# Quarter sums of two weights: a queue of their own and places of their own, in place

## The chip, the cores and the metric

The kernel runs on one core of one Trainium2 chip. The metric is the device time of one execution in microseconds (us). Before the change the median of three runs is 793.73 us (792.7 to 794.22).

## What is computed

```python
attn = softmax(cap * tanh(q @ k.T / sqrt(64) / cap))        # 4 x 12 heads, 448 tokens, 64 wide
x = (attn @ v) laid out as 1792 tokens x 768
h = ((x @ w1) * (x @ w2)) @ w3 @ w_out                       # 768 -> 1024 -> 1024 -> 768
h = h @ w_in                                                 # 768 -> 1024
solu = h * softmax(h)
ln = (solu - mean) / sqrt(var + 1e-6) * g_ln
out = ln @ w_out2                                            # 1024 -> 768
```

All inputs are float32. The kernel makes each float32 matmul from three products of a high and a low part (the high part is a cast to fp32r, the low part what remains): `THREE` names the pairs.

## The kernel before

The program has four stages, and TensorE works through them one after the other.

1. Attention runs by pairs of heads, and between its matmuls TensorE folds w3, w_out and w_in into one 1024 x 1024 weight (`fold`, L743), which lands in DRAM as `w_dr`. The order of all engines is written out there by a planner (`Order`) that keeps its own clock of what is due.
2. The gated products (`products`, L1108, matmul L1119) multiply the attention output by w1 and w2, in blocks f = 0 to 7 of 128 columns of each. The tokens come in four batches of 448; the first pass takes batches 0 and 1 for each f in turn, and a short second pass takes batches 2 and 3 for two blocks. A block's weight tile `wt` has two buffers; it is filled by three pieces of 512 columns (`plan_w`), each loaded as 512 KB into a landing tile `ld` (three of them), converted by three VectorE operations (L328, L331, L334) into one of two `cv` tiles, cast by ScalarE (L340, the high part) and subtracted by VectorE (L349, the low part). Piece 0 holds the columns that the block's first matmuls need. Once attention ends, about 365 us into the span, the order is no longer written out: the loop at L1304 emits 18 matmuls, then steps of the queues, and the framework's scheduler places the instructions of each engine, by its own estimate of when each can start, with the emission order as rank.
3. Six blocks (`multiply`, L1323) do the other batches with Strassen-like sums of tokens and weights: seven products each, whose operands are prepared beforehand. `first_set` combines the first block's weights (`set0`), `two_three` (T) and `one_four` (U) combine the tokens.
4. The last two weights (the folded `w_dr` and w_out2 times g_ln, `wg_dr`) are applied in the same manner (`product`, L1426), first with seven operands ws1 to ws7, later with seven wg.

A DRAM weight is taken as a 2 x 2 grid of quarters, and four of the seven operands need sums of quarters. These are made in stage 2: `plan_sums` loads all four quarters of one row block, subtracts four times on VectorE and stores four sums into `tw_dr` (t) or `tg_dr` (tg). Before the change each row block is done as two halves of the columns, so there are eight items t(0) to t(7) and eight items tg(0) to tg(7).

The work of stage 2 stands in queues of class `Ahead`: items are loaded up to `depth` ahead of the one in work, strictly in the order in which they were added. `ahead` holds almost all of it, `xq` the tokens. In `ahead`, after block 5's pieces: `plan_last(5)` (w_out2's block g5, converted through the same landing tiles and stored to `wg_dr`), set0's load, t(0) and t(1), block 6's pieces (w6), g6, t(2) to t(4), block 7's pieces (w7), g7, t(5) to t(7), `first_set`, tg(0) to tg(3), T, the load and split of ws1 (`plan_block`), tg(4) to tg(7), U, the load of ws2, set1. The sums land in the same three `ld` tiles as the weights, and their results go to four `ts` tiles. Each piece of w6 waits until block 4 is through, each of w7 until block 5 is.

All of these transfers but the tokens' factors (`rb`, issued by GpSimd) are issued by SP, in one queue. Besides the loads it carries the stores of the sums, of the products (`ab_dr`, L1147), of g (`wg_dr`, L655), and a 1.5 MB store of each block's split weight for later use (`w12_dr`, L1149).

Of the kernel before, what the change touches and what calls it, by code (L numbers as in the profile page):

```python
# [9 lines left out]
F32 = mybir.dt.float32  # L10
F32R = mybir.dt.float32r
U32 = mybir.dt.uint32
AF = mybir.ActivationFunctionType
ALU = mybir.AluOpType
# [4 lines left out]
P = 128  # L19
B, H, S, D = 4, 12, 448, 64  # L20
# [221 lines left out]
def attention_moe_solu(ctx: ExitStack, tc: tile.TileContext, q, k, v, cap, w12, w3t, wo, win, wout2, g_ln, out):  # L242
# [49 lines left out]
    ahead, xq = Ahead(LANDS, order), Ahead(1, order)  # L292
# [4 lines left out]
    def since(test):  # L297

        met = []

        def when():
            if not met and test():
                met.append(order.now)
            return met[0] if met else None
        return when

    def landing(i, src, n, kind):
        t = conv.tile([P, 2 * HALF], U32, tag="ld", bufs=LANDS, name=f"ld{i}")
        lands[i] = t[:, :n].bitcast(kind)
        dst = lands[i]  # L310
        if len(src.shape) == 3:
            dst = dst.rearrange("p (a b) -> p a b", a=src.shape[1])
        elif len(src.shape) == 4:
            dst = dst.rearrange("p (a b c) -> p a b c", a=src.shape[1], b=src.shape[2])
            for g in range(src.shape[1]):
                sync.dma_start(out=dst[:, g], in_=src[:, g])
            return
        sync.dma_start(out=dst, in_=src)
# [552 lines left out]
    def four(dr, i, part, n):  # L871

        return dr[i][:, :, :, part * n:(part + 1) * n]
# [4 lines left out]
    def summed(i, t_dr, i_, part, n, m, t):  # L878

        if m == 0:  # L880
            t.append(lands.pop(i).rearrange("p (g h n) -> p g h n", g=2, h=2))
        b = t[0]
        t.append(place["ts"].tile([P, HALF], F32, tag="ts", bufs=4, name=f"t{i}_{m}")[:, :2 * n].rearrange("p (t n) -> p t n", t=2))
        if m == 0:
            dve.tensor_tensor(t[1][:, 0], b[:, 0, 1], b[:, 0, 0], ALU.subtract)
            dve.tensor_tensor(t[1][:, 1], b[:, 1, 1], t[1][:, 0], ALU.subtract)
        else:
            dve.tensor_tensor(t[2][:, 0], b[:, 1, 1], b[:, 0, 1], ALU.subtract)
            dve.tensor_tensor(t[2][:, 1], b[:, 1, 0], t[1][:, 1], ALU.subtract)
        sync.dma_start(out=t_dr[2 * m:2 * m + 2, :, i_, part * n:(part + 1) * n].rearrange("t p n -> p t n"), in_=t[-1])  # L890

    def plan_sums(kind, dr, t_dr, i_, part, n):

        i = len(ahead.items)

        def rest():
            t = []
            for m in range(2):
                summed(i, t_dr, i_, part, n, m, t)
        ahead.add((kind, i_, part), lambda: landing(i, four(dr, i_, part, n), 4 * n, F32), list, lambda: [("none", 0, 0, 0, rest)], None, lambda: 0.0 if "ts" in place else None)  # L900
# [18 lines left out]

    def second(m):  # L920
        if m not in ws:
            ws[m] = both_.tile([P, 2, NF // 2, HALF], F32R, tag="many", name=f"ws{m}")
        return ws[m]

    def plan_block(m, part):
        there = since(lambda: "ws" in place)
        ahead.add(("f", m, part), lambda: block_load(m, part, W4, tw_dr, second(m)), list,
                  lambda: [("none", 0, 0, 0, lambda: block_split(ws[m], part))], None, there)
# [79 lines left out]
    def plan_plain(key, do, test, load=lambda: None):  # L1008
        ahead.add(key, load, list, lambda: [("none", 0, 0, 0, do)], None, since(test))
# [27 lines left out]
    halves_ = [(i_, part) for i_ in range(NF // 2) for part in range(2)]  # L1037

    def plan_t(*items):
        for k in items:  # L1040
            plan_sums("t", W4, tw_dr, *halves_[k], HALF // 2)

    def plan_tg(*items):
        for k in items:
            plan_sums("tg", G4, tg_dr, *halves_[k], DM // 4)
# [13 lines left out]
    plan_last(5)  # L1059
    plan_plain("set0", lambda: None, lambda: "set" in place, lambda: load_set(0))  # L1060
    plan_t(0, 1)
    plan_w(6)
    plan_last(6)
    plan_t(2, 3, 4)
    plan_w(7)
    plan_last(7)
    plan_t(5, 6, 7)
    plan_plain("first set", first_set, lambda: "set" in place and ("x", B - 1, NPAIR // 2 - 1) in xq.done)
    plan_tg(0, 1, 2, 3)
    for c in range(NC // 2):  # L1070
        plan_plain(("T", c), lambda c=c: two_three(c), lambda: (NF - 1, 0) in fin)
    for part in range(2):
        plan_block(EARLY[0], part)
    plan_tg(4, 5, 6, 7)
    for c in range(NC // 2):
        plan_plain(("U", c), lambda c=c: one_four(c), lambda: (NF - 1, 1) in fin)
    plan_plain(("f", EARLY[1]), lambda: None, lambda: "ws" in place, lambda: block_load(EARLY[1], None, W4, tw_dr, second(EARLY[1])))
# [221 lines left out]
    place["ws"] = ws = {EARLY[0]: wsp.tile([P, 2, NF // 2, HALF], F32R, tag="w1", name="ws1")}  # L1299
# [4 lines left out]
    while fill(18 * 201):  # L1304
        ahead.step(3)
        xq.step(1)
    while xq.step(1):
        pass
    while ahead.step(1):
        pass  # L1310
# [82 lines left out]
    for part in range(2):  # L1393
        plan(1 + part, 3, (high_w, ws, EARLY[1], part))
        plan(1 + part, 4, (low_w, ws, EARLY[1], part))
# [227 lines left out]
    plan(0, 3, (high_w, ws, 5, 0), (low_w, ws, 5, 0), (high_w, ws, 5, 1), (low_w, ws, 5, 1), (high, 0, 4), (high_w, ws, 4, 0), (sum4, 0))  # L1623
# [125 lines left out]
```

## Time and profile before

| | us |
|---|---|
| median of three runs | 793.73 |
| the profiled execution, its own time | 794.05 |
| its span, first to last instruction | 792.3 |
| TensorE busy | 772.7 |
| VectorE busy | 617.1 |
| ScalarE busy | 442.3 |

The span is what the instructions cover; the 1.75 us between it and the execution's time lie around it. Busy times are sums over the span: an engine can be 98% busy and still work at half its clock for a while, which the granted clock shows. An idle stretch has a releaser, the instruction or transfer that came last among those waited for. Names of tiles are the program's without their numbers, so the DRAM tensors `w_dr` and `w12_dr` both read `w_dr`, and `in_w12` reads `in_w`.

### The profile page before, as it was taken

What the parts mean: (1) busy time and instruction counts of PE and PEld (TensorE: products, weight loads), DVE (VectorE), ACT (ScalarE), POOL (GpSimd) and SP (SyncE); (2) the same over time, 40 slices, a digit from 0 to 9 for tenths busy, and PEclk for the clock granted to TensorE, in tenths of its full rate; (3) what the DMA queues carried; (4) which work ended last, traced back from release to release, by engine and by line L of the source; (5) the groups of instructions that cost most, each with busy time, mean ns of one, the idle gap of its engine ahead of it and who ended that gap; (6) DMA issues with size and microseconds to landing.
All of it is one profiled execution on the core that took longest, in us unless ns stands there. A gap on an engine that the chain in (4) does not pass through costs nothing.

```text
span 792.3 us, 11304 instructions
## 1 busy us (share of the span) xinstructions
PE 772.7 (98%) x3956; PEld 613.7 (77%) x3956; DVE 617.1 (78%) x1132; ACT 442.3 (56%) x656; POOL 55.0 (7%) x106
## 2 busy tenths in 40 slices
PE   9999999999999999999986998999999999999998
PEld 6546666876867676767986997998788888899998
DVE  6995795798999469965777978877886668978972
ACT  6887766357577767672222313324576666845642
POOL 0110000000110112001000000000011111100000
PEclk9999999999999999999998999999999999999999
DMA  8776465586996665647978797545743345996432
GB/s 288 249 226 225 126 216 171 183 259 224 324 316 219 217 207 180 187 160 270 326 269 303 247 308 248 168 149 181 238 151 115 107 99 130 274 198 132 138 93 80
DMA packets 150920, 162.46 MB, mean 205 GB/s; under 512 B 66324, under 2 KB 122832, under 8 KB 149840
## 3 DMA queue, kind: packets, MB, share of 16 engines
q1 hardware_dynamic: 148128, 155.91, 61.9%
q0 software_dynamic: 2592, 5.73, 2.9%
q8 instruction: 31, 0.51, 0.3%
q14 instruction: 25, 0.20, 0.1%
q10 hardware_dynamic: 144, 0.10, 0.0%
HBM read 114.04 MB, written 47.53 MB: 204 GB/s over the span
## 4 chain that ended last, share of the span: by engine, by line
PE 76%; DMA 9%; DVE 8%; ACT 4%; issue 2%; SPq 0%; DVEq 0%; ACTq 0%
PE u L1434 14%; PE o L523 9%; PE f L771 8%; PE f L755 8%; PE ab L1119 7%; PE v L1434 7%; PE sc L442 6%; PE us L1331 5%; PE y L1434 4%; PE n L523 2%; PE sc L438 2%; PE vs L1331 2%; DMA ld<-in_w 2%; DMA tg_dr<-t 2%; DMA ws<-w_dr 1%
## 5 line engine op out<-in xcount | busy, mean ns | idle before, releaser
L1119 PE MATMUL ab<-xs,wt 128*128 128x448 f32 x720 | 152.7, 370 | 8.3 <-ACT wt L340 8.3
L1119 PEld LDWEIGHTS ab<-xs,wt 128*128 128x128 f32 x720 | 137.2, 192 | 24.3 <-ACT wt L340 9.0
L455 ACT ACTIVATE sc<-sc,small 128x896 f32<-128x896 f32 (+1 forms) x96 | 82.8, 888 | 47.7 <-PE sc L442 42.0
L460 ACT ACTIVATE p<-sc,small 128x896 f32<-128x896 f32 (+1 forms) x96 | 84.5, 921 | 0.6
L1434 PE MATMUL u<-ws,a 128*128 128x512 f32 x336 | 80.7, 391 | 0.7 <-DVE ws L1375 0.5
L523 PE MATMUL o<-p,vd 128*64 128x448 f32 x384 | 77.5, 545 | 0.0
L1434 PEld LDWEIGHTS u<-ws,a 128*128 128x128 f32 x336 | 62.8, 188 | 15.0 <-DVE ws L1375 1.2
L755 PE MATMUL f<-w,w_o 128*128 128x512 f32 x288 | 70.7, 396 | 0.0
L771 PE MATMUL f<-w_i,w 128*128 128x512 f32 x288 | 68.1, 392 | 0.1
L755 PEld LDWEIGHTS f<-w,w_o 128*128 128x128 f32 x288 | 53.2, 188 | 16.3 <-issue 3.4
L771 PEld LDWEIGHTS f<-w_i,w 128*128 128x128 f32 x288 | 53.5, 188 | 14.2 <-issue 2.7
L1434 PE MATMUL u<-wg,a 128*128 128x384 f32 x336 | 62.0, 334 | 0.0
L1434 PEld LDWEIGHTS u<-wg,a 128*128 128x128 f32 x336 | 58.5, 188 | 0.4 <-DVE a L1569 0.3
L523 PEld LDWEIGHTS o<-p,vd 128*64 128x64 f32 x384 | 25.4, 136 | 41.2 <-issue 40.3
L334 DVE SCALAR_TENSOR_TENSOR cv<-ld,cv 128x512 uint32<-128x512 uint32 (+1 forms) x80 | 52.1, 658 | 0.8
L331 DVE SCALAR_TENSOR_TENSOR cv<-ld,cv 128x512 uint32<-128x512 uint32 (+1 forms) x80 | 51.9, 660 | 0.9
L1565 ACT CAST a<-s 128x512 fp32r<-128x512 f32 (+1 forms) x42 | 31.2, 755 | 30.5 <-DVE s L1587 17.9
L481 DVE TENSOR_TENSOR s<-p,p 128x896 f32<-128x896 f32 x18 | 19.6, 1091 | 32.8 <-ACT p L460 18.1
L328 DVE TENSOR_SCALAR cv<-ld 128x512 uint32<-128x512 uint32 (+1 forms) x80 | 32.2, 406 | 12.7 <-DMA ld<-in_w 6.0
L1434 PE MATMUL v<-ws,a 128*128 128x512 f32 x168 | 40.7, 390 | 0.5 <-DVE ws L1375 0.5
L1569 DVE TENSOR_TENSOR a<-s,a 128x512 fp32r<-128x512 f32 (+1 forms) x42 | 35.4, 851 | 6.5 <-ACT a L1565 6.4
L1434 PEld LDWEIGHTS v<-ws,a 128*128 128x128 f32 x168 | 31.5, 188 | 7.4 <-DVE ws L1375 0.9
(188 smaller groups left out, 1300.4 us busy)
## 6 DMA issues: line engine op xcount, KB each, us to landing
ld<-in_w SPq DMA_DIRECT2D x24, 512.0 KB, 5.0
w_dr<-wt SPq DMA_DIRECT2D x6, 1536.0 KB, 6.7
q<-w_dr SPq DMA_DIRECT2D x24, 384.0 KB, 4.1
ld<-in_w3t SPq DMA_DIRECT2D x16, 512.0 KB, 4.5
w_dr<-e SPq DMA_DIRECT2D x28, 256.0 KB, 3.5
ldx<-ab_dr SPq DMA_DIRECT2D x14, 512.0 KB, 4.1
c_dr<-h SPq DMA_DIRECT2D x14, 512.0 KB, 2.6
ldx<-c_dr SPq DMA_DIRECT2D x56, 128.0 KB, 3.2
```

The costliest lines, as they stand in the source:

```text
L331: dve.scalar_tensor_tensor(d[1], d[0][:, :, 1], 0xC0000000, d[1], ALU.bitwise_and, ALU.bitwise_or)
L334: dve.scalar_tensor_tensor(d[1], d[0][:, :, 0], 29, d[1], ALU.logical_shift_right, ALU.bitwise_or)
L442: pe.matmul(sc[:, j, :S], keys[rows], qq[rows, :], start=(m == 0), stop=(m == len(terms) - 1))
L455: act.activation(sc[:, :w, :S], sc[:, :w, :S], AF.Tanh, scale=qscale)
L460: act.activation(p, sc[:, :w, :S], AF.Exp, scale=capt)
L523: pe.matmul(dst[i * width:(i + 1) * width, :S], weights, moving, start=first, stop=stop)
L755: pe.matmul(banks_[c][0], lw[:, a], fw["3", h, g][:, e], start=begins, stop=(g == NF - 1 and m == 2))
L771: pe.matmul(begun_[m_][0], w34[m_][:, a, c, :], rw[:, e], start=(c == 0 and m == 0), stop=(c == NC - 1 and m == 2))
L1119: pe.matmul(pp[f, b, i][0][:, :S], w[:, u], xs[b, c][:, e], start=begins, stop=(c == NC - 1 and m == 2))
L1331: pe.matmul(pu[g], w[:, u, c * P:(c + 1) * P], moved(m, c)[:, e], start=(begins and c == 0 and i == 0), stop=(c == NC // 2 - 1 and i == 2) ...
L1434: pe.matmul(banks[g], a[r][m][:, p, k * P:(k + 1) * P], b[m][:, e, k, :], start=(first and k == 0 and i == 0), stop=(k == NF // 2 - 1 and ...
L1569: dve.tensor_tensor(lo, source(r, m), raw(hi), ALU.subtract)
```

## The change

- A third queue `tq` of depth 2 takes the sums, set0's load, T, `first_set`, U, the loads of ws2 and ws1, and set1. `ahead` keeps the blocks and g: after block 5's pieces come g5, g6, w6, g7, w7.
- Sums are made per row block at full width: four items t and four tg, each loaded by two transfers (each with both halves of one row of quarters), four subtractions in place (512 or 384 columns wide), two stores of two sums each.
- They land in places of their own: one tile `big` in the space of the former `ts` tiles, and two halves of the tile that later becomes ws1 (`within`). The order of places is big, half 0, half 1, big for t, and half 0, half 1, big, half 0 for tg.
- ws1 is loaded at the end of `tq`, and its split moves from stage 2 into blocks 3 and 4 of stage 3, in the steps where ws2's split stands in blocks 1 and 2.
- The loop of stage 2 takes 2 steps of `ahead`, 1 of `xq` and 2 of `tq` per 18 matmuls, where it took 3 and 1.
- In stage 4 the first half of ws5 is split one step sooner (step 2 of the first round).

```diff
-    ahead, xq = Ahead(LANDS, order), Ahead(1, order)
+    ahead, xq, tq = Ahead(LANDS, order), Ahead(1, order), Ahead(2, order)
...
-    def plan_sums(kind, dr, t_dr, i_, part, n):
-
-        i = len(ahead.items)
+    def plan_sums(kind, dr, t_dr, i_, n, home):
+
+        t = []
+
+        def load():
+            t.append(home(f"{kind}{i_}")[:, :4 * n].rearrange("p (g n) -> p g n", g=4))
+            for g in range(2):
+                sync.dma_start(out=t[0][:, 2 * g:2 * g + 2], in_=dr[i_][:, g])
 
         def rest():
-            t = []
-            for m in range(2):
-                summed(i, t_dr, i_, part, n, m, t)
-        ahead.add((kind, i_, part), lambda: landing(i, four(dr, i_, part, n), 4 * n, F32), list, lambda: [("none", 0, 0, 0, rest)], None, lambda: 0.0 if "ts" in place else None)
+            b = t.pop()
+            for to, x, y in ((0, 1, 0), (1, 3, 1), (3, 3, 0), (2, 2, 3)):
+                dve.tensor_tensor(b[:, to], b[:, x], b[:, y], ALU.subtract)
+            for m, two in ((0, b[:, ::3]), (2, b[:, 1:3])):
+                sync.dma_start(out=t_dr[m:m + 2, :, i_, :].rearrange("t p n -> p t n"), in_=two)
+        tq.add((kind, i_), load, list, lambda: [("none", 0, 0, 0, rest)], None, lambda: 0.0 if "ts" in place else None)
...
     def plan_plain(key, do, test, load=lambda: None):
-        ahead.add(key, load, list, lambda: [("none", 0, 0, 0, do)], None, since(test))
+        tq.add(key, load, list, lambda: [("none", 0, 0, 0, do)], None, since(test))
...
+    def apart(name):
+        return place["ts"].tile([P, 4 * HALF], F32, tag="big", name=name)
+
+    def within(k):
+        def home(name):
+            if "first" not in homes:
+                homes["first"] = wsp.tile([P, 2, 4 * HALF], F32, tag="w1", name="sums")
+            return homes["first"][:, k]
+        return home
+
+    def begin_weight(m):
+        ws[m] = (wsp if m == EARLY[0] else both_).tile([P, 2, NF // 2, HALF], F32R, tag="w1" if m == EARLY[0] else "many", name=f"ws{m}")
+        block_load(m, None, W4, tw_dr, ws[m])
...
-    plan_last(5)
+    for f in range(5, NF):
+        plan_last(f)
+        if f > 5:
+            plan_w(f)
+    for i_, home in enumerate((apart, within(0), within(1), apart)):
+        plan_sums("t", W4, tw_dr, i_, HALF, home)
     plan_plain("set0", lambda: None, lambda: "set" in place, lambda: load_set(0))
-    plan_t(0, 1)
-    plan_w(6)
-    plan_last(6)
-    plan_t(2, 3, 4)
-    plan_w(7)
-    plan_last(7)
-    plan_t(5, 6, 7)
-    plan_plain("first set", first_set, lambda: "set" in place and ("x", B - 1, NPAIR // 2 - 1) in xq.done)
-    plan_tg(0, 1, 2, 3)
     for c in range(NC // 2):
         plan_plain(("T", c), lambda c=c: two_three(c), lambda: (NF - 1, 0) in fin)
-    for part in range(2):
-        plan_block(EARLY[0], part)
-    plan_tg(4, 5, 6, 7)
+    for i_, home in enumerate((within(0), within(1))):
+        plan_sums("tg", G4, tg_dr, i_, DM // 2, home)
+    plan_plain("first set", first_set, lambda: "set" in place and ("x", B - 1, NPAIR // 2 - 1) in xq.done)
+    for i_, home in enumerate((apart, within(0))):
+        plan_sums("tg", G4, tg_dr, i_ + 2, DM // 2, home)
     for c in range(NC // 2):
         plan_plain(("U", c), lambda c=c: one_four(c), lambda: (NF - 1, 1) in fin)
-    plan_plain(("f", EARLY[1]), lambda: None, lambda: "ws" in place, lambda: block_load(EARLY[1], None, W4, tw_dr, second(EARLY[1])))
+    for m in EARLY[1::-1]:
+        plan_plain(("f", m), lambda: None, lambda: "ws" in place, lambda m=m: begin_weight(m))
...
     while fill(18 * 201):
-        ahead.step(3)
+        ahead.step(2)
         xq.step(1)
+        tq.step(2)
...
-    for part in range(2):
-        plan(1 + part, 3, (high_w, ws, EARLY[1], part))
-        plan(1 + part, 4, (low_w, ws, EARLY[1], part))
+    for m, n in ((EARLY[1], 1), (EARLY[0], 3)):
+        for part in range(2):
+            plan(n + part, 3, (high_w, ws, m, part))
+            plan(n + part, 4, (low_w, ws, m, part))
...
-    plan(0, 3, (high_w, ws, 5, 0), (low_w, ws, 5, 0), (high_w, ws, 5, 1), (low_w, ws, 5, 1), (high, 0, 4), (high_w, ws, 4, 0), (sum4, 0))
+    plan(0, 2, (high_w, ws, 5, 0), (low_w, ws, 5, 0))
+    plan(0, 3, (high_w, ws, 5, 1), (low_w, ws, 5, 1), (high, 0, 4), (high_w, ws, 4, 0), (sum4, 0))
```

## Rows read from the trace of the kernel before

**Rows 1.** The page: TensorE's busy time, then its busy tenths in 40 slices

```profile
PE 772.7 (98%) x3956; PEld 613.7 (77%) x3956; DVE 617.1 (78%) x1132; ACT 442.3 (56%) x656; POOL 55.0 (7%) x106
...
PE   9999999999999999999986998999999999999998
```

**Rows 2.** Waits of TensorE, 370 to 600 us: total, times, longest

```profile
PE ab L1119 <- ACT wt L340: 8.3, 2, 6.3
PE vs L1331 <- ACT p7s L1335: 2.8, 1, 2.8
PE u L1434 <- DVE ws L1375: 0.5, 1, 0.5
PE v L1434 <- DVE ws L1375: 0.5, 1, 0.5
```

**Rows 3.** Windows: us, busy PE, PEld, DVE, ACT, POOL; PE clock, DMA share, GB/s

```profile
372.00:385.00 13.00, 13.00 (x66) 12.19 (x66) 8.39 (x17) 3.85 (x7) 2.03 (x5) 1.00 0.82 219
385.00:400.00 15.00, 14.79 (x74) 13.52 (x73) 11.47 (x23) 5.05 (x8) 1.29 (x3) 1.00 1.05 370
400.00:424.00 24.00, 16.25 (x72) 14.67 (x72) 18.91 (x39) 5.54 (x10) 0.00 (x0) 0.89 0.79 276
...
sum 98.00, PE 89.72 PEld 82.87 DVE 79.19 ACT 27.91 POOL 3.31; mean PE 17.94 PEld 16.57 DVE 15.84 ACT 5.58 POOL 0.66
```

**Rows 4.** Timeline, 370 to 445 us: start, length, instruction, idle before it and releaser

```profile
369.82 29.97 PE L1119 MATMUL ab<-xs,wt 128*128 128x448 f32 x149
...
399.22 0.43 DVE L328 TENSOR_SCALAR cv<-ld 128x512 uint32<-128x512 uint32 x1 [2.44 <-DMA ld<-in_w]
...
401.80 16.25 PE L1119 MATMUL ab<-xs,wt 128*128 128x448 f32 x72 [2.01 <-ACT wt L340]
...
408.07 0.69 DVE L334 SCALAR_TENSOR_TENSOR cv<-ld,cv 128x512 uint32<-128x512 uint32 x1
...
421.53 0.43 DVE L328 TENSOR_SCALAR cv<-ld 128x512 uint32<-128x512 uint32 x1 [2.76 <-DMA ld<-in_w]
...
424.32 20.86 PE L1119 MATMUL ab<-xs,wt 128*128 128x448 f32 x92 [6.28 <-ACT wt L340]
```

**Rows 5.** Timeline of SP's queue: set0, ws1, block 5's store, w6, w7

```profile
373.10 2.62 SPq L942 DMA_DIRECT2D q<-w_dr  x4
376.10 0.90 SPq L914 DMA_DIRECT2D ws<-w_dr  x2
...
386.41 0.32 SPq L1149 DMA_DIRECT2D w_dr<-wt  x1
...
389.25 0.33 SPq L318 DMA_DIRECT2D ld<-in_w  x1
...
415.52 0.36 SPq L318 DMA_DIRECT2D ld<-in_w  x1
```

**Rows 6.** Transfers issued at 389.25 and at 415.52: size, us to landing

```profile
ld<-in_w SPq DMA_DIRECT2D x1, 512.0 KB, 9.9
...
ld<-in_w SPq DMA_DIRECT2D x1, 512.0 KB, 6.0
```

**Rows 7.** VectorE by line and shape, 370 to 485 us: busy, mean ns, idle before

```profile
L349 DVE TENSOR_TENSOR wt<-cv,wt 128x512 fp32r<-128x512 f32 x9 | 6.2, 686 | 1.0 <-ACT wt L340 1.0
...
L885 DVE TENSOR_TENSOR t<-ld 128x256 f32<-128x256 f32 x8 | 3.4, 419 | 1.6 <-DMA ld<-w_dr 1.6
...
L885 DVE TENSOR_TENSOR t<-ld 128x192 f32<-128x192 f32 x8 | 2.8, 353 | 1.7 <-DMA tg_dr<-t 1.6
```

**Rows 8.** Transfers issued at 472.8 and 473.5; timeline: what waited for the second

```profile
ws<-w_dr SPq DMA_DIRECT2D x1, 1024.0 KB, 7.8
ab_dr<-abs SPq DMA_DIRECT2D x1, 224.0 KB, 7.7
...
481.30 0.53 ACT L1335 COPY p7s<-vs 128x448 f32<-128x448 f32 x1 [5.24 <-DMA ab_dr<-abs]
```

**Rows 9.** Timeline, 545 to 605 us: VectorE on ws5's halves

```profile
559.35 2.36 DVE L1375 TENSOR_TENSOR ws<-ws 128x1024 fp32r<-128x1024 f32 x2 [2.68 <-ACT ws L1371]
```

More of the change, by code (lines that the diff above doesn't have):

```diff
@@ L876, in attention_moe_solu @@
     G4 = wg_dr.rearrange("(g i) h p n -> i p g h n", g=2)
[L878 to L890, printed above, removed]
-    def plan_sums(kind, dr, t_dr, i_, part, n):
-        i = len(ahead.items)
-        def rest():
-            t = []
-            for m in range(2):
-                summed(i, t_dr, i_, part, n, m, t)
-        ahead.add((kind, i_, part), lambda: landing(i, four(dr, i_, part, n), 4 * n, F32), list, lambda: [("none", 0, 0, 0, rest)], None, lambda: 0.0 if "ts" in place else None)
+    def plan_sums(kind, dr, t_dr, i_, n, home):
[4 more added lines that the diff above has]
+                sync.dma_start(out=t[0][:, 2 * g:2 * g + 2], in_=dr[i_][:, g])
+        def rest():
+            b = t.pop()
[4 more added lines that the diff above has]
+        tq.add((kind, i_), load, list, lambda: [("none", 0, 0, 0, rest)], None, lambda: 0.0 if "ts" in place else None)
     def rows(part):
@@ L918, in block_split @@
         split(hi, lo, raw(lo))
[L920 to L928, printed above, removed]
     sets, tx, AGAIN = {}, {}, NF - 2
@@ L1035, in one_four @@
         split(t4[:, 0], t4[:, 1], t)
[L1037 to L1045, printed above, removed]
+    homes = {}
+    def apart(name):
[9 more added lines that the diff above has]
+        block_load(m, None, W4, tw_dr, ws[m])
     plan_w(0)
@@ L1298, in attention_moe_solu @@
     wsp = opened(right, "ws", "right")
-    place["ws"] = ws = {EARLY[0]: wsp.tile([P, 2, NF // 2, HALF], F32R, tag="w1", name="ws1")}
+    place["ws"] = ws = {}
     opened(right, "under", "right").tile([P, 48], F32, name="under")
@@ L1309, in attention_moe_solu @@
     while ahead.step(1):
+        pass
+    while tq.step(1):
         pass
```

## The prediction

> **What bounds the kernel now.** I read the page first: TensorE is busy 772.7 us of 792.3 [rows 1], so nothing is to be won except in its gaps, and the slices show where these are: two weak slices just past the middle (8 and 6 tenths) and a small dent (8) three slices further on. The wait list of TensorE for 370 to 600 us names them [rows 2]: 8.3 us in two waits of the gated products (L1119) for the high cast of a weight block (L340), 2.8 us of the blocks stage for the copy p7s, and two waits of 0.5 us for the splits of L1375 in the last stage. Everything that the change edits lies in or just behind these places.
>
> The timeline gives the two large ones [rows 4]. Up to 399.79 us 149 matmuls take 29.97 us, 0.2011 us each. Block f=6 then starts 2.01 us late, at 401.80, and its 72 matmuls take 16.25 us where 72 x 0.2011 = 14.48: 1.77 us lost to a clock that fell in the stall (granted 0.89 in 400 to 424 us [rows 3]). f=7 starts 6.27 us late, at 424.32, and the next 92 matmuls take 20.86 us instead of 92 x 0.2011 = 18.50, 2.36 us too many. Together 2.01 + 1.77 + 6.27 + 2.36 = **12.4 us**, the stake of this change in the gated stage.
>
> Why were the weights late? Each time VectorE's first conversion (L328) waits for the landing, and TensorE starts 2.6 to 2.8 us after it [rows 4]. The first piece of f=6 was issued at 389.25 and needed 9.9 us; the 1.5 MB store of block 5 (L1149) was issued just ahead of it, and set0, ws1 and the first sums before that [rows 5, 6]. The first piece of f=7 was issued only at 415.52 and needed 6.0 us [rows 5, 6]: its landing tile ("ld", three of them) was held by the sums t(2) to t(4), which stand between block 6 and block 7 in the queue `ahead`. So f=6 is late by the transfer queue, f=7 by the ring of landing tiles. The change takes the sums out of that ring; it doesn't take their bytes out of the transfers.
>
> **The change part by part.**
> *Ring (f=7).* In `ahead` now stand g5, g6, w6, g7, w7 with nothing between. w7's first piece takes the tile of w6's third, whose conversion ended at 408.76 [rows 4]. If f=6 comes 2.5 us later (below), that is 411.3; with the 6.0 us of [rows 6] it lands at 417.3. TensorE would reach f=7 at 404.3 + 14.48 + 1.77 = 420.5 and needs the landing 2.8 us ahead, by 417.7. So the stall of 6.27 us and its 2.36 us of slow clock go: -8.6 us. What is late next is f=6.
>
> *Burst (f=6).* From 373.1 us, where SP may first load into the freed space [rows 5], three sums (t0, t1, t2, 1.05 MB each) now go out at once ahead of set0, where one (as two halves) went before; g6 (0.79 MB) also moves ahead of w6, ws1 (1.05 MB) moves out. Net 2 x 1.05 + 0.79 - 1.05 = 1.84 MB more before w6's first piece. At the 370 GB/s of 385 to 400 us [rows 3] that is 5.0 us. Against it, 372 to 385 us moved only 219 GB/s [rows 3]; filled up to 370 that stretch would hold 13 x 151 = 1.96 MB more, all of it. So w6 lands between 399.2 (no loss) and 404.2, or 407.0 if t0's stores (1.05 MB) are ahead of it too. Below zero is possible as well: VectorE no longer sits before set0's landing, so g5 is converted and w6 issued sooner. I take +2.5 us, in the middle: the issues at 376 us and later were already queued (the stretch behind them runs full), so the slack is partly a start-up, not room. f=6 then starts at 404.3, 4.5 us late, and still pays 1.77: 6.3 us remain of 12.4, **-6.1 us**.
>
> The Trainium skill ("DMA: Bandwidth & Descriptors", section "Issuing engines are not separate DMA queues") says that transfers end up on the same 16 DMA engines and interleave, whoever starts them; a queue of one's own in the program is then none in the transfers. By that rule the 5.0 us would be due in full and f=6 would start at 406.8 (the third rival below, with its chance). The 9.9 us of w6 behind other traffic [rows 6] agree with it.
>
> *VectorE.* The four subtractions per piece go from 64 narrow ones to 32 wide ones: now 32 x 0.419 + 32 x 0.353 = 24.7 us [rows 7]; at 512 columns 0.686 us [rows 7] and at 384, on the line between the rows, 0.553: 16 x 0.686 + 16 x 0.553 = 19.8. That is -4.9 us, and ws1's split (two subtractions like the pair of 2.36 us in [rows 9]) leaves the stage. VectorE is busy 79.2 us of these 98 [rows 3], so this is room and no time: I count 0. It guards a stage shortened by 6 us (72 of 92 us). The wait that the change adds on VectorE is that of t1 and t2 for loads of 1 MB; behind it in VectorE's order stand the conversions of g5, g6 and w6 and the products' evictions. Its price is part of the burst above, since w6 waits for the same transfers; alone it costs nothing while block 5's 14.5 us of matmuls cover it. The wait of t3 for t0's stores holds back sums alone.
>
> *ws1 in the blocks stage.* Two ScalarE casts and two VectorE subtractions move to blocks 3 and 4, at the steps where ws2's already stand in blocks 1 and 2; no wait of those blocks appears in [rows 2], so 0, and at worst 1.2 us, one such subtraction, once.
>
> *End of the gated stage.* The 2.8 us: p7s waits for the landing of the last abs store, 7.7 us after its issue, behind a 1 MB load of ws2 and stores of sums [rows 8]. The sums are earlier now, but ws1 and ws2 both close the new queue. Bounds: all 2.8 gained, or another 1.05 MB ahead, 2.8 lost. I take **-1.4**.
>
> *Last stage.* ws5's first half is split one step sooner, in a stretch where VectorE then waited 2.68 us [rows 9]. The two waits for L1375 are 1.0 us; **-0.7** is taken. If the load were not there, ScalarE would block: +1 us at most.
>
> Sum: -6.1 - 1.4 - 0.7 = -8.2. Against the profiled execution's own 794.05 us that is 785.85; it lies 0.3 above the median of 793.73, so **785.5 us**.
>
> **The rivals.**
> *Both stalls go (777.5).* The loads fit into the slack of 372 to 385 us and w6, issued sooner, lands by 397.2: -12.4 - 2.8 - 1.0 = -16.2. For it: 1.96 MB of room against 1.84 MB. Against it: the queue is one, in order, and critical pieces stand behind the sums.
>
> *The burst eats the gain (slower, 798).* Place: f=6. The stores of t0 and t1 (2.1 MB) as well as the loads stand ahead of w6: 3.94 MB, 10.6 us, landing 409.8, start 412.4, 12.6 us late plus 1.8 of clock. The stores of t2 and the load of t3 (2.1 MB, 5.7 us) come before its second and third pieces; some 3 us of that, half, I let outlast what the first piece feeds. 12.6 + 1.8 + 3 = 17.4 instead of 12.4, less 0.7: +4.3. It decides from a landing of w6 at about 407 us on. For it: these pieces have rank over w6 in program order, and the sum of the bytes is the same as before. Against it: stores need their sums, and those need landings.
>
> *It moves the stall, no more (792).* w6 lands at the 404.2 of the full queue, so f=6 loses 7.0 + 1.8 us, and its second piece, behind stores, costs another 3: 11.8 instead of 12.4, and about 1 of the small gains. For it: the same bytes must pass before f=7. Against it: 400 to 424 us moved only 276 GB/s [rows 3]. This is also the case in which the change doesn't do what it says: instructions outside the hand-written order are placed by a planner that takes them when it thinks them ready (ws1 went out at 376.10 [rows 5], though it is written behind most of the sums), so a separate queue may change the order little.
>
> **How the numbers follow.** 0.2% of 793.7, 1.6 us, is about what a measurement of this kernel can tell from no change: 792.1 to 795.3. Chances: forecast (780.5 to 790) 0.40, both stalls gone 0.22, moved only 0.20 (0.15 of it inside 1.6 us, 0.05 faster), burst 0.18. Faster 0.67, same 0.15, slower 0.18. The range goes from 776.5, which leaves out nearly half of the second case, to 798, which leaves out half of the last: under 2 in 10.
>
> **What would show it.** Right: TensorE's wait for L340 once, at f=6, of 3 to 6 us, none at f=7; w7's first load issued before 413 us; landings of w6 at 400 to 404 us; transfers nearly full from 374 to 400; p7s waiting less. Wrong: both waits gone with w6 landing by 397; or f=6 starting after 409; or a new wait of the products for tokens or of block 0 for the first set, with VectorE full ahead of it.

## The result and the profile after

The changed kernel takes 798.03 us (median of four runs, 797.47 to 798.8) where the kernel before took 793.22 beside it: ratio 1.0061, 95% interval 1.0044 to 1.0079, so it is slower by about 4.8 us. (In the rounds of experiments below the kernel before had medians of 793.7 to 794.2 in 52 executions.) The forecast was 785.5. The number is that of the burst rival (798), and its place, f=6, is one of the two places; but of the difference to the forecast two thirds came at f=7, where that rival, too, had no loss.

The profiled execution has a span of 796.2 us, 3.9 above that of before. TensorE's waits for 350 to 620 us, the counterpart of [rows 2]:

```profile
PE ab L1107 <- ACT wt L340: 13.4, 2, 8.1
PE u L1426 <- DVE ws L1366: 0.7, 2, 0.5
...
```

Both waits for weights are still there and are 5.1 us longer together; the 2.8 us of p7s are gone. The timeline has them in place (start, length, instruction, idle before and its releaser), with VectorE's conversion of block 6's first piece; compare [rows 4]:

```profile
366.43 34.28 PE L1107 MATMUL ab<-xs,wt 128*128 128x448 f32 x170
...
405.86 0.43 DVE L328 TENSOR_SCALAR cv<-ld 128x512 uint32<-128x512 uint32 x1 [6.87 <-DMA ld<-in_w]
...
408.86 16.38 PE L1107 MATMUL ab<-xs,wt 128*128 128x448 f32 x72 [8.14 <-ACT wt L340]
...
430.46 46.22 PE L1107 MATMUL ab<-xs,wt 128*128 128x448 f32 x216 [5.23 <-ACT wt L340]
...
476.52 1.96 PE L1322 MATMUL us<-xs,q 128*128 128x448 f32 x9
```

At the undisturbed 0.2011 us per matmul, 72 are 14.48 us and 216 are 43.44. So f=6 costs 8.14 + 1.90 of slow clock, f=7 costs 5.23 + 2.78: 18.05 us where the kernel before lost 12.4. From the first pure row of products to the blocks stage it is 110.09 us instead of 104.42. That is the ledger's main term; the whole of it, in spans:

| stretch | before | after | difference |
|---|---|---|---|
| start of the pure products | 365.51 | 366.43 | +0.92 |
| gated stage from there | 104.42 | 110.09 | +5.67 |
| blocks stage | 79.26 | 76.19 | -3.07 |
| last stage, to the end of its first waits | 21.95 | 22.34 | +0.39 |
| the rest | 221.16 | 221.15 | 0 |

The first line is no effect of the change: in the runs below that start lies anywhere from 364.4 to 368.1. In windows (us, busy PE, PEld, DVE, ACT, POOL, PE clock, DMA share, GB/s), after first, then the last line of before, which [rows 3] does not have:

```profile
385.00:400.00 15.00, 15.00 (x77) 14.06 (x76) 13.02 (x24) 3.23 (x6) 1.29 (x3) 1.00 1.03 398
400.00:424.00 24.00, 15.86 (x71) 14.18 (x70) 16.84 (x30) 5.19 (x9) 0.00 (x0) 0.86 1.05 399
...
440.00:470.00 30.00, 30.00 (x151) 28.07 (x150) 23.30 (x43) 9.18 (x18) 0.00 (x0) 1.00 0.48 162
```

```profile
440.00:470.00 30.00, 30.00 (x151) 28.02 (x151) 26.78 (x64) 8.33 (x16) 0.00 (x0) 1.00 0.88 277
```

The transfers ran full up to 440 us (373 GB/s in the stretch left out here, share 0.99), and then stood half idle. From 372 to 490 us the windows give 33.6 MB before and 32.8 after: nearly the same bytes were moved, only sooner, and the weights that TensorE waited for were among them. SP's queue shows in which order (start, length, transfer, count), in two stretches, then the sizes and times to landing of the transfers issued at 393.18 and 417.47:

```profile
374.07 0.89 SPq L885 DMA_DIRECT2D t<-w_dr  x2
375.32 1.97 SPq L885 DMA_DIRECT2D sums<-w_dr  x4
377.33 3.45 SPq L925 DMA_DIRECT2D q<-w_dr  x4
381.75 3.98 SPq L318 DMA_DIRECT2D ld<-in_wout  x2
386.70 0.33 SPq L1135 DMA_DIRECT2D ab_dr<-abs  x1
387.99 0.33 SPq L655 DMA_DIRECT2D wg_dr<-wg  x1
389.06 0.32 SPq L1137 DMA_DIRECT2D w_dr<-wt  x1
390.12 1.42 SPq L892 DMA_DIRECT2D tw_dr<-t  x2
392.22 0.36 SPq L892 DMA_DIRECT2D tw_dr<-sums  x1
393.18 0.35 SPq L318 DMA_DIRECT2D ld<-in_w  x1
...
406.85 1.55 SPq L885 DMA_DIRECT2D t<-w_dr  x2
...
412.63 3.32 SPq L885 DMA_DIRECT2D sums<-wg_dr  x4
416.89 0.35 SPq L318 DMA_DIRECT2D ld<-in_wout  x1
417.47 0.35 SPq L318 DMA_DIRECT2D ld<-in_w  x1
```

```profile
ld<-in_w SPq DMA_DIRECT2D x1, 512.0 KB, 12.6
...
ld<-in_w SPq DMA_DIRECT2D x1, 512.0 KB, 7.8
```

Block 6's first piece goes out at 393.18, behind six loads of sums and three of their stores, and lands at 405.8; before it was issued at 389.25 and landed at 399.2 [rows 5, 6]. Block 7's first piece goes out at 417.47, behind t3's loads and the four of tg0 and tg1, and lands at 425.2, exactly when f=6 ends.

### The profile page after: what moved, and what is told of

It is laid out like the page before. It is cut to its first block, busy times and chain, and to the rows that moved or that the text cites. A ratio compares the mean times of both kernels' runs of the same rounds, so it can differ in the third digit from the quotient of the medians.

```text
span 796.2 us, 11216 instructions
## 1 busy us (share of the span) xinstructions
PE 773.2 (97%) x3956; PEld 614.1 (77%) x3956; DVE 615.2 (77%) x1100; ACT 441.5 (55%) x656; POOL 55.5 (7%) x106
## 4 chain that ended last, share of the span: by engine, by line
PE 85%; DMA 5%; ACT 4%; DVE 4%; issue 2%; SPq 0%; DVEq 0%; ACTq 0%
PE ab L1107 15%; PE u L1426 14%; PE o L523 9%; PE f L771 8%; PE f L755 8%; PE v L1426 7%; PE sc L442 6%; PE us L1322 5%; PE y L1426 4%; PE vs L1322 2%; PE n L523 2%; PE sc L438 2%; DMA ld<-in_w 2%; PE ys L1322 1%; DMA sums<-w_dr 1%
```

## The experiments

Three theories stand against each other. **T1**: the sums' transfers stand ahead of blocks 6 and 7 in SP's queue (SP is SyncE, which issues almost all transfers; w6 and w7 are the two blocks' weights). **T2**: VectorE is held by waits for the sums' landings, so the conversions come late. **T3**: it is one of the moved pieces (ws1's split, ws5's step). The table gives what all runs are compared by; the gated stage is measured as above, the waits are TensorE's in f=6 (its 72 matmuls) and behind it, f=7 first.

| kernel | median, us | ratio to before, 95% | gated stage | f=6 | behind it |
|---|---|---|---|---|---|
| before | - | - | 104.42 | 2.01 | 6.28 |
| changed | 798.03 | 1.0061 [1.0044, 1.0079] | 110.09 | 8.14 | 5.23 |
| e1_one_place | 790.04 | 0.9968 [0.9944, 0.9992] | 99.57 | 5.07 | 0.64 |
| e2_no_subs | 800.44 | 1.0083 [1.0051, 1.0114] | 112.38 | 6.55 + 3.71 | 3.68 |
| e7_pool | 803.07 | 1.0106 [1.0073, 1.0139] | 111.97 | 4.74 + 0.69 + 0.20 | 9.76 |
| e6_behind67 | 783.87 | 0.9876 [0.9847, 0.9905] | 96.68 | 2.12 | 0.28 + 0.85 + 0.17 |
| e10_t3_behind7 | 789.89 | 0.9958 [0.9941, 0.9975] | 102.63 | 8.34 | 0.16 |
| e11_stores_late | 793.21 | 0.9996 [0.9975, 1.0017] | 107.65 | 5.56 | 3.50 + 2.04 |
| e4_ws1_late | 793.15 | 1.0000 [0.9984, 1.0017] | 104.68 | 0.41 + 0.92 | 8.48 |
| e3_ws5_only | 793.45 | 0.9998 [0.9977, 1.0019] | 104.57 | 2.35 + 1.04 | 6.37 |
| e8_t0_too | 786.00 | 0.9914 [0.9899, 0.9929] | 94.24 | 1.11 + 0.21 | 0.27 |
| e9_set0_too | 783.37 | 0.9878 [0.9864, 0.9893] | 95.33 | 0 | 0.64 + 0.89 + 1.10 |
| e12_e9_ws5_back | 782.70 | 0.9854 [0.9826, 0.9882] | 95.54 | 0 | 0.90 + 0.88 + 1.11 |

458 matmuls at 0.2011 us are 92.1 us, the floor of the gated stage. Of e11 a second execution is shown (the reason is told there). How far single waits move between executions shows in e3, which has the code of the kernel before in this stage: its wait at f=6 is 2.35 + 1.04 us instead of 2.01, at f=7 6.37 instead of 6.28, and p7s waits 2.07 instead of 2.79.

**One landing place instead of three (e1_one_place).** The sums keep their queue and their form, but t1 must wait for t0's stores.

```diff
-    for i_, home in enumerate((apart, within(0), within(1), apart)):
+    for i_, home in enumerate((apart, apart, apart, apart)):
```

(and the same in the two loops of tg)

> The changed kernel, but all eight sums use the one place big, so each sum's loads wait for the stores of the sum before. T1 (the sums' transfers stand ahead of w6 and w7 in SP's queue): 1 MB instead of 3 MB goes out ahead of w6, which lands some 5 us sooner than in the changed kernel; f=6 starts by 403 us instead of 408.9, f=7 waits under 2 us instead of 5.2; 784 to 790 us. T2 (VectorE, in order, is held by waits for the sums' landings): also better, since only one sum waits there early, 786 to 792. T3 (the moved split of ws1, the place of g6 and g7, or ws5's step cost the time): still 796 to 799, f=6 at 408 or later.

Measured 790.04. Of the sums only t0 now goes ahead of block 6, but with it the 1 MB load of ws1, whose place no sum takes any more (issued at 376.98). f=6 waits 5.07 us, starting at 404.64 and not by 403, and f=7 0.64:

```profile
PE ab L1107 <- ACT wt L340: 5.1, 1, 5.1
```

So fewer early sums mean shorter stalls, and the rest of the change is worth something: the gated stage is 4.85 us shorter than before. Three waits for p7s, now on VectorE, keep the blocks stage at 79.41 us.

**VectorE without the subtractions (e2_no_subs).**

```diff
-            for to, x, y in ((0, 1, 0), (1, 3, 1), (3, 3, 0), (2, 2, 3)):
-                dve.tensor_tensor(b[:, to], b[:, x], b[:, y], ALU.subtract)
```

> The changed kernel without the subtractions of the sums: VectorE does none of them, the quarters are loaded and stored as they are, so the kernel leaves out that part of the computation. The transfers stay. T1: the queue is as full as before, f=6 is 5 to 9 us late and f=7 waits 3 us or more: 794 to 799 us. T2: nothing on VectorE waits for the sums' loads, both waits shrink to 2 us or less together: 784 to 788 us. T3: 796 to 799 us.

Measured 800.44, above the changed kernel and above all three ranges. Nothing of VectorE's work on the sums or of its waits for these landings is left, and the stalls add up to more: the stores, which no longer wait for a subtraction, go out sooner still: four of them, not three, stand ahead of block 6's first piece, and two more with t3's loads between its first and its second. So T2 alone does not make the loss. At f=6 the changed kernel's own trace rules it out: VectorE stood idle 6.87 us before block 6's first conversion, waiting for the landing. At f=7 VectorE's order has a share (below).

**The sums' transfers in GpSimd's queue (e7_pool).**

```diff
-                sync.dma_start(out=t[0][:, 2 * g:2 * g + 2], in_=dr[i_][:, g])
+                pool.dma_start(out=t[0][:, 2 * g:2 * g + 2], in_=dr[i_][:, g])
...
-                sync.dma_start(out=t_dr[m:m + 2, :, i_, :].rearrange("t p n -> p t n"), in_=two)
+                pool.dma_start(out=t_dr[m:m + 2, :, i_, :].rearrange("t p n -> p t n"), in_=two)
```

> The changed kernel with the loads and stores of the sums issued by GpSimd, in its own queue; the same bytes at the same readiness. T1 as a matter of the place in SP's queue: w6 is no longer held by places of the sums, it shares the engines; f=6 starts by 404, f=7 waits under 3: 785 to 792 us. T1 as a matter of bytes alone: the engines are as full, f=6 at 406 or later: 794 to 800. Risk: the tokens' factors (rb) stand behind the sums in GpSimd's order, a new wait of the products for tokens of batch 3, 1 to 5 us. T2: VectorE waits for the same landings, 795 to 799.

Measured 803.07, beyond all three ranges, though no new wait for tokens appears (the profiled execution, 798.39, is its shortest). Out of SP's queue the sums are still in the way: block 6's first piece, issued at 389.20, needs 11.7 us and lands at 400.9 instead of 405.8. The loss moves to f=7:

```profile
403.88 11.97 PE L1107 MATMUL ab<-xs,wt 128*128 128x448 f32 x48 [4.74 <-ACT wt L340]
...
431.86 45.13 PE L1107 MATMUL ab<-xs,wt 128*128 128x448 f32 x216 [9.76 <-ACT wt L340]
```

At f=6, then, it is not SP's order alone, but what is in flight at all. The Trainium skill ("DMA: Bandwidth & Descriptors", section "Issuing engines are not separate DMA queues") says that transfers from any engine end up on the same 16 DMA engines and interleave; this run agrees: landings of the two queues take turns (SP 400.91, GpSimd 401.13, SP 402.62, GpSimd 402.87), and from 400 to 424 us the engines were 0.99 busy.

More than half of the 9.76 us at f=7 is VectorE's. Block 7's first piece landed at 423.51, 1.4 us after f=6 ended, but was first touched 4.8 us later:

```profile
428.27 0.41 DVE L328 TENSOR_SCALAR cv<-ld 128x512 uint32<-128x512 uint32 x1
```

From 420.31 on VectorE does the subtractions of t3, tg0 and tg1 and the conversions of g7 ahead of it, without an idle stretch. From landing to TensorE's start it is 8.35 us, where the kernel before has 2.8.

**The sums behind the blocks (e6_behind67).** t0 as it was; t1 and t2 may load only when block 6's last piece is converted, t3 and tg behind block 7. A one-column copy from that piece's tile into the landing place makes the load wait; set0 goes ahead of the sums.

```diff
-        plan_sums("t", W4, tw_dr, i_, HALF, home)
+        plan_sums("t", W4, tw_dr, i_, HALF, home, (None, 6, 6, 7)[i_])
...
+            if behind is not None:
+                for g in range(2):
+                    dve.tensor_copy(t[0][:, 2 * g, :1], raw(wt[behind][:, 1, -1:]))
```

> The changed kernel with real dependences: t1, t2 may only be loaded after block 6's weights are split (a copied column ties them), t3 and all tg only after block 7's; set0 goes first. T1: w6 stands behind 1 MB of sums and set0 as before the change, f=6 starts at 400 to 402.5; w7's first piece has no sum ahead, f=7 waits under 1.5 us: 781 to 787 us, unless the sums then crowd the first blocks of the next stage (then 787 to 792). T2: the same direction, less. T3: 796 to 799.

Measured 783.87, 1.2% below the kernel before and 14 us below the changed one, with every other part of the change in place. The gated stage is 96.68 us, the clock 1.00 throughout:

```profile
366.37 39.22 PE L1110 MATMUL ab<-xs,wt 128*128 128x448 f32 x194
407.70 9.88 PE L1110 MATMUL ab<-xs,wt 128*128 128x448 f32 x48 [2.12 <-ACT wt L340]
```

T1 is right in sign and size. What the run leaves open: which of the sums make which stall, loads or stores, and what the subtractions do, which move behind the blocks together with the transfers.

**Only t3 and tg behind block 7 (e10_t3_behind7).** SP's order is the changed kernel's up to block 6's three pieces; set0 goes ahead of t3.

```diff
+        plan_sums("t", W4, tw_dr, i_, HALF, home, (None, None, None, 7)[i_])
...
+        plan_sums("tg", G4, tg_dr, i_, DM // 2, home, 7)
```

> The changed kernel with t0, t1, t2 as they are, and t3 and all of tg loaded only behind block 7's last piece. SP's order is the changed kernel's up to block 6's three pieces. Theory T1 (transfers that stand ahead of a block's pieces in SP's order make it late): f=6 waits 8 us as in the changed kernel, f=7 waits under 1 us instead of 5.2 and its clock does not fall, so 8 us of stall and clock go; up to 2.8 us come back at the end of the gated stage, since later transfers stand in front of its last store: 789 to 793 us. Rival T4 (f=7 is late because f=6 was late, and whatever order the transfers have makes no difference): f=7 still waits 4 us or more, 796 to 799 us.

Measured 789.89, in the middle of T1's interval. f=6 keeps its stall, f=7 loses its own and the slow clock behind it:

```profile
407.38 17.18 PE L1111 MATMUL ab<-xs,wt 128*128 128x448 f32 x76 [8.34 <-ACT wt L340]
424.72 42.83 PE L1111 MATMUL ab<-xs,wt 128*128 128x448 f32 x212 [0.16 <-DVE wt L349]
```

So t0, t1, t2 make f=6's stall, and t3 with tg0 and tg1, transfers and subtractions together, makes f=7's: it was not the first stall that made the second. The p7s wait did not come back.

**Loads early, stores late (e11_stores_late).** Here the loads of t0 to t2 go out as in the changed kernel, but the subtractions, and so the stores, hang on block 6's last piece. (Not shown: `tq` has depth 4 until that piece is done, and set0 stands ahead of t3.)

```diff
+            if kind == "t" and i_ < 3:
+                dve.scalar_tensor_tensor(b[:, 0, :1], raw(wt[6][:, 1, -1:]), 0.0, b[:, 0, :1], ALU.mult, ALU.add)
```

> The changed kernel with the loads of t0, t1, t2 as early as there, but their subtractions and stores tied to block 6's last piece (one more small VectorE instruction for each); set0 ahead of t3, and t3 and tg behind the stores. It tells loads from stores in what made f=6 late. T1, with the stores' share: the three stores (1.5 MB) that stood ahead of block 6's first piece are 3.9 us at 398 GB/s, so that piece lands at about 402 instead of 405.8, and TensorE's wait at f=6 is 3.5 to 5 us instead of 8.1; at f=7 under 1 us. 785 to 790 us. Rival (the loads alone do it): f=6 still waits 7 us or more.

The median is 793.21, 5 us under the changed kernel, but the profiled execution was the longest of its ten (798.29, the products starting only at 368.06) with a wait of 7.53 us at f=6. So it was run again, with the changed kernel.

> The kernel whose stores of t0 to t2 are tied to block 6's last piece, once more, since its profiled execution (798.3 us) was the longest of its ten (median 793.2) and can't speak for them. T1 with the stores' share: in an execution of about 793 us TensorE waits 3.5 to 5.5 us at f=6. Rival (the loads alone do it): 7 us or more again, and the shorter time comes from f=7 or from behind it.

> The same kernel a third time, for the spread of its first stall: as above, 3.5 to 5.5 us at f=6 by T1, 7 us or more by the rival.

> The changed kernel once more, for the spread of its two stalls between executions: its times lie within 1.4 us of each other, so 8.1 and 5.2 us should come again within 1 us each. If they move by 2 us or more, one profile of it can't carry the terms.

They took 792.51, 795.12 and, for the changed kernel, 796.76 us (one execution each; the kernel before took 797.39 beside them, so their times compare with no others here; their waits do). The changed kernel's two waits came again as 8.14 and 5.23, to the digit; those of e11 vary: 5.56 and 6.18 at f=6. From the first of the two:

```profile
404.96 16.35 PE L1115 MATMUL ab<-xs,wt 128*128 128x448 f32 x72 [5.56 <-ACT wt L340]
424.81 1.19 PE L1115 MATMUL ab<-xs,wt 128*128 128x448 f32 x4 [3.50 <-ACT wt L340]
428.04 44.89 PE L1115 MATMUL ab<-xs,wt 128*128 128x448 f32 x212 [2.04 <-DVE wt L349]
```

Neither side is right as it stands. Without the stores f=6 waits 0.6 to 2.6 us less, not 3.9; the loads alone leave it at 5.6 to 7.5 where the kernel before waits 2.0. So of the added 6 us some 4 are loads and some 2 are stores. The saving is smaller than the stores' bytes since the stretch moved less without them: 371 GB/s from 385 to 400 us (345 and 334 in the other two) against 398. Why a queue with fewer stores moves less stays open. And f=7's 5.5 us here are VectorE's: block 7's first piece landed at 415.3, was first touched at 417.07, and its three conversions end at 424.1, with the late subtractions between them:

```profile
417.07 0.42 DVE L328 TENSOR_SCALAR cv<-ld 128x512 uint32<-128x512 uint32 x1
...
417.88 1.28 DVE L892 TENSOR_TENSOR sums<-sums 128x512 f32<-128x512 f32 x2
...
419.68 0.68 DVE L331 SCALAR_TENSOR_TENSOR cv<-ld,cv 128x512 uint32<-128x512 uint32 x1
...
422.82 0.68 DVE L892 TENSOR_TENSOR t<-t 128x512 f32<-128x512 f32 x1
423.42 0.68 DVE L334 SCALAR_TENSOR_TENSOR cv<-ld,cv 128x512 uint32<-128x512 uint32 x1
```

**ws1's split alone (e4_ws1_late).** The kernel before, with the split moved to blocks 3 and 4.

```diff
-    for part in range(2):
-        plan_block(EARLY[0], part)
...
+    for m, n in ((EARLY[1], 1), (EARLY[0], 3)):
```

> The kernel before with one part of the change alone: ws1's split in blocks 3 and 4 of the blocks stage instead of the gated stage; its 1 MB load goes out where it did before (around 376 us). T1: the split is VectorE work that nothing waits for in either place, so f=6 and f=7 wait 8.3 us together as before and the blocks stage keeps its length: 792.5 to 795 us. T3 (the moved split is what costs): blocks 3 and 4 get new waits of 1.2 to 2.4 us, 795 to 797 us.

Measured 793.15, no difference. ws1's load went out at 376.90, as before the change. Blocks 3 and 4 got no wait, so T3 falls for this part. The two stalls changed places (1.3 us at f=6, 8.5 at f=7), with the same sum to a microsecond and a half: f=7 starts 59.3 us into the stage here and 58.8 before, so with f=6 in time it only waits the longer for weights that come no sooner. The blocks stage is 76.80 us instead of 79.26, since p7s waits 0.3 us instead of 2.8.

**ws5's step alone (e3_ws5_only).**

```diff
+    plan(0, 2, (high_w, ws, 5, 0), (low_w, ws, 5, 0))
-    plan(0, 3, (high_w, ws, 5, 0), (low_w, ws, 5, 0), (high_w, ws, 5, 1), (low_w, ws, 5, 1), (high, 0, 4), (high_w, ws, 4, 0), (sum4, 0))
+    plan(0, 3, (high_w, ws, 5, 1), (low_w, ws, 5, 1), (high, 0, 4), (high_w, ws, 4, 0), (sum4, 0))
```

> The kernel before with the one step of the last stage alone: the first half of ws5 split one step sooner. By the prediction the waits for the splits in the first round fall from 1.0 us by 0.7: the first round is 0.7 us shorter. Rival T5 (the split then stands ahead of another one that is due sooner): the first round gets longer by 0.4 us, as in the changed kernel. In the time both are within what a measurement can tell, 792.5 to 795 us; the waits in the trace decide.

In the time nothing, as expected; in the trace the first round is 20.81 us, 1.14 shorter than before, and one wait for the splits is left instead of two:

```profile
PE u L1434 <- DVE ws L1375: 0.3, 1, 0.3
```

So the step gains where it stands alone, and in the changed kernel it does not: there the round is 22.34. VectorE's rows say what differs. In e3 ws5's first half is split at 554.95, 7.4 us into the round; in the changed kernel at 563.23, 10.5 us into it, behind a token operand for which VectorE idled 3 us:

```profile
562.01 0.69 DVE L1561 TENSOR_TENSOR a<-s,a 128x512 fp32r<-128x512 f32 x1 [3.03 <-ACT a L1557]
...
563.23 2.39 DVE L1366 TENSOR_TENSOR ws<-ws 128x1024 fp32r<-128x1024 f32 x2
```

The code asks for the earlier step in both; in the trace it comes later in the changed kernel. Why, no run tells.

**More behind the blocks (e8_t0_too, e9_set0_too, e12_e9_ws5_back).** e8 sends t0 behind block 6 as well, e9 set0 too, e12 is e9 with ws5's step as it was before the change. (In e9 a copied column ties set0's place to block 6's last piece, too.)

```diff
-        plan_sums("t", W4, tw_dr, i_, HALF, home, (None, 6, 6, 7)[i_])
+        plan_sums("t", W4, tw_dr, i_, HALF, home, (6, 6, 6, 7)[i_])
...
-    plan_plain("set0", lambda: None, lambda: "set" in place, lambda: load_set(0))
+    plan_plain("set0", lambda: None, lambda: "set" in place and ("w", 6, 2) in ahead.done, lambda: load_set(0))
```

> As the kernel in which t1, t2 stand behind block 6 and t3, tg behind block 7 (783.9 us), with t0 behind block 6 too. T1: t0's loads and stores, 2.1 MB or 5.3 us at 398 GB/s, leave the front of block 6's pieces, so f=6's remaining waits (2.1, 0.3 and 0.9 us) go: 780.5 to 783 us. Rival (moved work is then late at the end): the last sums and tokens' combinations come late, p7s or the first block waits 3 us or more: 784 to 787 us.

> As the kernel with t0, t1, t2 behind block 6 and t3, tg behind block 7, with set0's 1.5 MB behind block 6 too. T1: no stall is left at f=6 that set0 could cause, so nothing more is gained: within 1 us of the kernel with t0 behind block 6. Rival (the first block needs set0 early): its combination comes late, the blocks stage starts 1.5 us or more later.

> As the kernel with t0, t1, t2 and set0 behind block 6 and t3, tg behind block 7 (783.4 us), with ws5's first half split in the step of the kernel before. If the earlier step costs the 0.4 us that the changed kernel's first round is longer, 782.5 to 783.5 us; if it gains, 783.5 to 784.5 us. The waits of the first round decide.

e8 takes 786.00, by the medians 2 us more than e6, though the intervals just overlap. In the gated stage T1 holds (94.24 us instead of 96.68), but the blocks stage is 81.02 us instead of 77.65: what was pushed back now stands ahead of the last abs store, which needs 9.1 us to land, and p7s waits 2.98 us instead of 1.19, with a slow clock behind it:

```profile
471.72 3.05 PE L1325 MATMUL vs<-t,q 128*128 128x448 f32 x9 [2.98 <-ACT p7s L1329]
```

That is the rival of this run. In e9 the same wait is 0.4 us, and TensorE's first 326 matmuls of the stage run without any gap, past the starts of f=6 (after 170) and f=7 (after 242):

```profile
365.16 65.51 PE L1112 MATMUL ab<-xs,wt 128*128 128x448 f32 x326
```

e9 takes 783.37 us, 2.6 less than e8, where no more than 1 us was expected. e12 takes 782.70: the intervals overlap, and the first round is 22.52 us in e12, 22.34 in e9, so ws5's step decides nothing here. (What makes this round 0.4 us longer than before is neither ws5's step, by e12, nor ws1's move, by e4 with 21.95; no run shows what it is.) Both lie 1.2 to 1.5% below the kernel before, and by the medians some 15 us below the changed one.

## Why the prediction was wrong

**What bounded the kernel: right in the main.** f=6 late by the transfer queue, f=7 by a landing tile. e8 and e9 show that 9 to 10 of those 12.4 us could be had (104.42 to 94.24 and 95.33). One thing was overlooked: in the kernel before, f=6's first piece, too, went out only when its landing tile came free, at 389.25. VectorE held it: its last conversion of g5, which ends at 389.23, stood behind the wait for set0 and a subtraction of ws1's split:

```profile
388.68 0.55 DVE L334 SCALAR_TENSOR_TENSOR cv<-ld,cv 128x384 uint32<-128x384 uint32 x1
```

In e4, without that split, the piece left as soon as the queue let it, and f=6 waited 0.41 us for it.

**Burst (f=6): a term sized too small.** The text had the range right (no loss to 404.2 by the loads, 407.0 with t0's stores) and took 2.5 us "in the middle" because 372 to 385 us moved only 219 GB/s. The landing came at 405.8, 6.6 us later (5.7 into a stage that began 0.9 later), and f=6 costs 10.0 us, not 6.3. Most of that room was not there for these transfers. The same windows from 374 us on, before and after:

```profile
374.00:385.00 11.00, 11.00 (x56) 10.31 (x56) 6.39 (x14) 2.71 (x5) 1.34 (x2) 1.00 0.94 249
```

```profile
374.00:385.00 11.00, 11.00 (x57) 10.31 (x56) 9.67 (x18) 3.23 (x7) 1.62 (x2) 1.00 0.97 292
```

Already before, the DMA engines were 0.94 busy there, at 249 GB/s: slow transfers, not missing ones. The 0.82 of [rows 3] came from the first two microseconds. With the sums in SP's queue the change found 11 x 43 GB/s = 0.47 MB of the 1.96 MB that the text counted. The busy share is not the last word either: in e7, with the sums in GpSimd's queue, the same stretch moved 371 GB/s at a share of 0.99. Why the transfers were slower with SP's queue alone, no run shows. The Trainium skill ("Perfetto Trace Analysis", section "Identifying the Most-Contended Engine") advises to judge DMA by how much of the memory's peak it moves, and not by occupancy; here neither number alone told how much room the stretch had. The rule of the Trainium skill that the prediction quoted, by which it took the 5.0 us as due in full, gave the better term: the loads cost about 4. The other half of the error is the stores, which the text left to the top of its range and to a rival; e11 puts them at 0.6 to 2.6 us.

**Ring (f=7): the step that failed most.** -8.6 us was taken, -0.6 came (8.01 us where 8.6 stood); that is two thirds of the miss. No sum held the tile any more, as the text says, but it came free at 416.91 and not at 411.3, since block 6's third piece came late with the first, and block 7's first piece went out at 417.47, after the 413 that the text named as the sign:

```profile
416.23 0.68 DVE L334 SCALAR_TENSOR_TENSOR cv<-ld,cv 128x512 uint32<-128x512 uint32 x1
```

That lateness alone makes no stall, because TensorE was late at f=6 by as much: in e10 the piece goes out at 415.46, 11.1 us after block 6's first conversion began as against 11.6 in the changed kernel, and f=7 waits 0.16 us. What failed are the two terms behind the issue, which the text carried over from the kernel before. The 6.0 us to landing of [rows 6] became 7.8 (3.5 in e10): t3, tg0 and tg1 (2.6 MB of loads) had taken the sums' old place in SP's queue between the blocks and were under way ahead of the piece. And the 0 for VectorE was too little: the piece is there at 425.24, and in the chain of waits between it and TensorE's start lie conversions of g7 and subtractions of tg:

```profile
425.36 0.59 DVE abs L1126
425.95 0.47 DVE sums L890
426.42 0.27 DVE cv L328
```

In the kernel before it is 2.8 us from the first conversion to the start [rows 4], so 2.4 of the 5.23 us are VectorE's and 2.8 the landing's. e10 takes away the transfers and the subtractions together; the division between them is read from this one trace, and no run tests it.

**ws1's split: right** in the sum, at 0 (e4). **End of the gated stage: right in sign,** -1.4 taken, -2.8 and its clock came: with the transfers done early, nothing stood ahead of the last abs store, which landed 1.9 us after its issue. But it needs no burst: in e4, with the sums where they were, p7s waits 0.3 us, against 2.8 before and 2.1 in e3. **Last stage: wrong here,** -0.7 taken, +0.39 came, though the step alone gives -1.14 (e3).

**The rivals.** "The burst eats the gain" gave 17.4 us of stalls and clock; 18.05 were measured. Its sum is nearly right, its parts are not: it had a landing at 409.8 and no stall at f=7, and by its own mark (407 at f=6) the measured 405.8 lies on the other side. What carried the loss over the line is the second stall. The range ended at 798.0, just short of the time, and that the rival's number fits so well is luck. Behind both stalls stands the same omission: the prediction wrote out SP's new order, item by item, for block 6 alone, and there took half of the price; for block 7 it followed tiles alone and put neither the sums' transfers nor their subtractions ahead of the piece.

## What to carry to other kernels

Work that is not urgent and gets a place of its own will start as soon as the place is free, and its transfers then stand ahead of the urgent ones; a free buffer is no reason to load. Tie such loads to the last urgent piece (here a one-column copy), which made 798 us into 783, and look at what the pushed-back transfers then delay (e8). Before counting room in a stretch, read its busy share beside its GB/s (here 0.94 at 249), and write out what will stand ahead of each urgent piece, in the queue and on the engine that converts it, down to the last consumer.

## What was not expected of the hardware

**Eight transfers of SP's queue were under way at a time.** In the queue of the changed kernel above, count from the first load of q (issued 377.33): four of q, two of g, abs, wg are eight, and the ninth, the 1.5 MB store, goes out at 389.06. That first q landed 11.7 us after its issue, at 389.0:

```profile
q<-w_dr SPq DMA_DIRECT2D x1, 384.0 KB, 11.7
```

The next three go out at 390.12, 391.17 and 392.22, where q's others land at 390.06, 391.11 and 392.16. The waits of SP (total, times, longest) name them, though those stores have nothing to do with q:

```profile
SPq L892 <- DMA q<-w_dr: 1.9, 3, 0.7
```

So in a full queue each piece is issued when the one eight places ahead has landed, and in this queue it lands 7 to 13 us later, whether it has 192 KB or 1.5 MB. That is where the 12.6 us of block 6's piece come from: seven transfers of 4.0 MB together stood before it, and with its own 0.5 MB that is an estimated 11 us at the 398 GB/s of the stretch. In none of the traces did SP's queue hold more than eight, and its transfers always landed in order of issue. Whether the chip or the framework sets the eight, no run tells.

**A stall of 2 us did not always cost clock.** The 2.01 us at f=6 before were followed by 16.25 us for 72 matmuls (14.48 at full speed), the 2.12 us in e6 by 9.88 for 48 (9.65). The granted clock was 0.5 from 402 to 405 us in the kernel before, and 1.00 all through the stage in e6. e3, with the code of before, stalled 2.35 us at the same place and kept a clock of 1.00. What decides between them is open.
